# A recurrence and a gated two-layer network in one kernel: engines of 453 elementwise steps and the order of all steps read from two tables

## The chip, the cores and the metric

The kernel runs on one core of one Trainium2 chip. The core has a matrix engine (TensorE, PE in the rows; its weight loads are PEld), three elementwise engines (VectorE = DVE, ScalarE = ACT, GpSimd = POOL) and a queue that starts transfers (SyncE = SP). The metric is the device time of one execution in microseconds; lower is better.

## The reference

Per head, a state of 48 x 48 is decayed and updated once per position and read by a query; the result, brought to 3072 tokens of 384, goes through two matrix products with an activation between them. All inputs and outputs are float32.

```python
def _attn_ref(q, k, v, f_logit):                    # 4, 8, 768, 48
    f = 1.0 / (1.0 + np.exp(-f_logit))
    for t in range(S):
        state = f[:, :, t, :, None] * state + np.einsum('bhd,bhe->bhde', k[:, :, t], v[:, :, t])
        y[:, :, t] = np.einsum('bhd,bhde->bhe', q[:, :, t], state)
...
def _moe_ref(x, w_in, w_out):                       # 3072 x 384, 384 x 2048, 2048 x 384
    h = x @ w_in
    sp = np.where(h > 20.0, h, np.log1p(np.exp(np.minimum(h, 20.0))))
    g = h * np.tanh(sp)
    return g @ w_out
```

## The kernel before

**The recurrence** is done in 24 chunks of 128 positions (numbered n; one chunk holds half of the heads of two batches, and four chunks in a row make up one group of 512 tokens). `prep` makes the decays of a chunk (clamp, exp and ln on ACT, running sums on PE for chunks 0 to 2 and by a scan on DVE after that), and multiplies k by `inv` and q by `dec`, in `times`. `attn0` makes the scores and masks them into `a`; `attn1` transposes k into `kt`; `attn2` makes the two halves of the state update, of which `mid` and `tmp` are the results in the middle and at the end of the chunk; `attn3` and `outputs_of` make the outputs, and `evict` brings them to `xt` (group 0 goes through `xs`, which lies in the space named spareh) and decays the state on POOL.

**The network** is done in 98 units (numbered u): for one group of 512 tokens and one of 16 blocks of 128 hidden columns, PE makes `h` (L317; L327 for the first five blocks, where weights and tokens are not split into two parts), a chain of elementwise steps makes `g` from `h`, and PE adds `g` times the second weights into `o` (L365; L330 for the first blocks). The chain of `mish` is: exp (ACT, L351), clamp and add (DVE, L352), square (DVE, L344; ACT, L343, for the first 24 units), ln and exp (ACT, L354 and L355), `g` (DVE, L356, which also reads `h`), a copy `gh` into the short float type fp32r (ACT, L358) and the rest `gl` (POOL, L348; DVE, L347, for the first 24 units). PE multiplies `gh` and `gl` apart, so that products keep float32's precision. `h` has two buffers, so the product of unit u+2 waits until the step `g` of unit u has read its `h`; the output product of a unit is issued two units after its `h`.

**The weights** come as 64-bit words with the value in all of them. `load_w` brings a block of them together with one step on ACT (L476) and three on DVE (L478, L479, L481), and `split_w` splits it into `wh` (ACT, L493) and `wl` (DVE, L494). All 16 blocks are converted once, during the first third of the program.

**The order.** The kernel does not run its steps as it makes them. Each call of `plan.add` records a step with its engine, an assumed cost and the buffers that it reads and writes; there are 1813 steps. `Plan.order` packs them with a list scheduler that honours engines, buffers and the port that DVE and POOL share (`port`), perturbs the ranks with some 300 seeds of `MOVES`, and keeps the best. `Plan.issue` then writes the instructions out in the order of the planned starts. Each engine works off its own instructions strictly in that order. While PE is planned to wait, in the beginning, `issue` puts in a multiplication of zeros that keeps the engine busy (`idle`, L462); there are 26 of them, each of which shows as two matmuls in the rows.

## Time and profile before

| | us |
|---|---|
| median of 3 runs | 486.04 |
| lowest, highest | 484.88, 486.46 |
| the profiled execution | 484.71 |
| its span, first to last instruction | 482.9 |

1.8 us of the profiled execution lie around its span, and it is 1.33 us (0.27%) under the median. The clock of TensorE was granted in full (0.996 over the span), so no stretch is told apart by it. A row of windows gives the busy time of each engine in a stretch of the span; a row of a timeline gives start, duration, engine, line, output and inputs, and in brackets how long the engine stood idle just before and what released it. Durations of neighbours on DVE and ACT overlap by some 0.08 us, so what an instruction costs its queue is the distance from its start to the start of the next, where nothing waits between them.

### The profile page before, as it was taken

The numbers are of one execution on the slowest core, as the hardware profiler recorded it, in microseconds if no ns is written. First come the engines' busy times: TensorE is split into PE (matmuls) and PEld (weight loads), VectorE is DVE, ScalarE is ACT, GpSimd is POOL, SyncE is SP. The second block draws the span as 40 slices with busy tenths as digits, with TensorE's granted clock in tenths as the row PEclk, the third lists the DMA queues.
The fourth block names the chain that finished last, engine by engine and source line by source line (L and its number), as shares of the span: only waits on it lengthen the run. The fifth ranks groups of instructions, "written<-read, shape, count | busy, mean of one in ns | idle before, by whom it ended". The sixth has DMA issues, their size and how long they took to land.

```text
span 482.9 us, 12157 instructions
## 1 busy us (share of the span) xinstructions
PE 464.4 (96%) x5032; PEld 391.2 (81%) x5032; DVE 343.8 (71%) x600; ACT 352.8 (73%) x662; POOL 144.3 (30%) x126
## 2 busy tenths in 40 slices
PE   8988989899999999999999999999999999999994
PEld 8766547787778888888888888888888888888883
DVE  4579999999996878777676766865875554554551
ACT  6779887999989677667777787677676466665650
POOL 0411120000013354343543443343333233342431
PEclk9999999999999999999999999999999999999998
DMA  7776656453402253421211240220230000010001
GB/s 246 226 252 222 222 183 220 140 178 118 160 36 89 93 188 106 154 70 63 89 50 73 88 139 16 90 88 33 90 110 1 3 12 23 1 65 0 1 0 71
DMA packets 17102, 48.42 MB, mean 100 GB/s; under 512 B 2000, under 2 KB 2000, under 8 KB 17040
## 3 DMA queue, kind: packets, MB, share of 16 engines
q1 hardware_dynamic: 17040, 47.59, 28.9%
q8 instruction: 40, 0.66, 0.5%
q14 instruction: 22, 0.18, 0.1%
HBM read 39.32 MB, written 6.29 MB: 94 GB/s over the span
## 4 chain that ended last, share of the span: by engine, by line
PE 71%; DVE 13%; ACT 12%; issue 3%; DVEq 0%; ACTq 0%
PE o L365 30%; PE h L317 30%; DVE wt L479 2%; PE at L755 2%; DVE ng L356 2%; ACT ng L354 2%; PE at L762 1%; ACT ng L355 1%; ACT ng L343 1%; DVE wl L494 1%; PE at L609 1%; DVE gl L347 1%; ACT wt L476 1%; PE o L462 1%; PE h L582 1%
## 5 line engine op out<-in xcount | busy, mean ns | idle before, releaser
L317 PE MATMUL h<-xt,wh 128*128 128x512 f32 x546 | 164.2, 382 | 3.7 <-DVE ng L356 3.7
L348 POOL TENSOR_TENSOR gl<-ng,gh 128x512 fp32r<-128x512 f32 x74 | 100.6, 1362 | 174.4 <-ACT gh L358 153.4
L317 PEld LDWEIGHTS h<-xt,wh 128*128 128x128 f32 x546 | 101.6, 189 | 21.3 <-DVE ng L356 7.0
L356 DVE SCALAR_TENSOR_TENSOR ng<-ng,h 128x512 f32<-128x512 f32 x91 | 62.1, 684 | 63.6 <-ACT ng L355 63.0
L365 PE MATMUL o<-gh,wh 128*128 128x512 f32 x273 | 106.3, 389 | 0.0
L365 PE MATMUL o<-gl,wh 128*128 128x512 f32 x273 | 103.6, 379 | 0.5 <-DVE gl L347 0.5
L317 PE MATMUL h<-xt,wl 128*128 128x512 f32 x273 | 103.5, 379 | 0.0
L365 PE MATMUL o<-gh,wl 128*128 128x512 f32 x273 | 103.5, 379 | 0.0
L354 ACT ACTIVATE ng<-ng 128x512 f32<-128x512 f32 (+1 forms) x98 | 60.7, 620 | 35.3 <-DVE ng L344 31.1
L351 ACT ACTIVATE ng<-h 128x512 f32<-128x512 f32 (+1 forms) x98 | 57.3, 585 | 31.9 <-PE h L317 30.9
L358 ACT ACTIVATE gh<-ng 128x512 fp32r<-128x512 f32 x91 | 56.6, 625 | 22.3 <-PE o L365 14.6
L352 DVE TENSOR_SCALAR ng<-ng 128x512 f32<-128x512 f32 (+1 forms) x98 | 47.9, 489 | 30.0 <-ACT ng L351 29.5
L355 ACT ACTIVATE ng<-ng 128x512 f32<-128x512 f32 (+1 forms) x98 | 60.6, 619 | 2.4
L411 POOL TENSOR_TENSOR in<-in,inv 128x512 f32<-128x512 f32 x20 | 24.9, 1244 | 119.6 <-ACT inv L548 119.5
L365 PEld LDWEIGHTS o<-gl,wh 128*128 128x128 f32 x273 | 51.6, 189 | 8.2 <-DVE gl L347 0.9
L365 PEld LDWEIGHTS o<-gh,wh 128*128 128x128 f32 x273 | 51.6, 189 | 7.9 <-issue 0.2
L317 PEld LDWEIGHTS h<-xt,wl 128*128 128x128 f32 x273 | 51.6, 189 | 7.3
L365 PEld LDWEIGHTS o<-gh,wl 128*128 128x128 f32 x273 | 51.6, 189 | 6.8 <-issue 0.2
L344 DVE TENSOR_TENSOR ng<-ng 128x512 f32<-128x512 f32 x74 | 54.7, 739 | 2.2
L542 DVE TENSOR_TENSOR_SCAN inv<-gate,state 128x516 f32<-128x516 f32 x20 | 24.6, 1228 | 2.3 <-ACT gate L533 2.1
L780 POOL TENSOR_TENSOR state<-tmp,ends 128x192 f32<-128x192 f32 x20 | 14.7, 735 | 19.0 <-PE at L755 7.9
L479 DVE SCALAR_TENSOR_TENSOR wt<-raw,wt 128x768 int32<-128x768 int32 x16 | 17.9, 1119 | 0.2
(147 smaller groups left out, 571.7 us busy)
## 6 DMA issues: line engine op xcount, KB each, us to landing
in<-lk SPq DMA_DIRECT2D x18, 512.0 KB, 4.4
raw<-ww SPq DMA_DIRECT2D x12, 768.0 KB, 4.2
in<-qv SPq DMA_DIRECT2D x18, 512.0 KB, 4.2
out<-ob SPq DMA_DIRECT2D x18, 256.0 KB, 2.1
raw<-ww SPq DMA_DIRECT2D x8, 384.0 KB, 4.4
in<-lk SPq DMA_DIRECT2D x8, 256.0 KB, 3.6
in<-qv SPq DMA_DIRECT2D x8, 256.0 KB, 4.2
xt<-xt SPq DMA_DIRECT2D x15, 128.0 KB, 3.0
```

The lines of the kernel that those rows point to most:

```text
L317: nc.tensor.matmul(h, w[:, a * P : (a + 1) * P], read(xt[:, x, a], part), start=(n == 0), stop=(n == 3 * NK - 1))
L344: ("dve", T_DVE(w), 1, lambda: nc.vector.tensor_tensor(n, n, n, ALU.mult))
L348: ("pool", T_POOL(w), 1, lambda: nc.gpsimd.tensor_tensor(gl, g, gh.bitcast(F32), ALU.subtract))
L351: ("act", T_ACT(w, True), 0, lambda: nc.scalar.activation(n_out, h, AF.Exp)),
L352: ("dve", T_DVE(w / 2), 1, lambda: nc.vector.tensor_scalar(n, n, E_CAP, 1.0, ALU.min, ALU.add)),
L354: ("act", T_ACT(w), 0, lambda: nc.scalar.activation(g, n, AF.Ln, bias=0.5, scale=0.5)),
L355: ("act", T_ACT(w), 0, lambda: nc.scalar.activation(g, g, AF.Exp, scale=-1.0)),
L356: ("dve", T_DVE(w), 0, lambda: nc.vector.scalar_tensor_tensor(g_out, g_in, 1.0, h, ALU.subtract, ALU.mult)),
L358: ("act", T_ACT(w), 0, lambda: nc.scalar.activation(gh, g, AF.Copy)),
L365: nc.tensor.matmul(o, w, read_again(x), start=(first and i == 0), stop=(last and i == 2))
L411: add("pool" if on_pool else "dve", cost, lambda: eng.tensor_tensor(dst, x, y, ALU.mult), reads, writes, port=port)
L479: add("dve", T_DVE(W_TILE), lambda: nc.vector.scalar_tensor_tensor(t, low, 29, t, ALU.logical_shift_right, ALU.bitwise_or), [kr], [kt], po ...
```

## The change

The list scheduler and its seeds are gone. `Plan.order` reads the order of all 1813 steps from a table, `ORDER`, and keeps only the arithmetic of planned starts, on which the fillers of `issue` depend. A second table, `CHOICES`, has one digit for each of 453 steps that may run on one of two engines; `Plan.either` takes the engine from it. Such steps are the square, `gh` and `gl` of each unit, `wh` and the split of `xs`, the two products of `times` (q only from chunk 9 on), the copies out of PSUM (`kt`, `mid`, `xs`, the upper part of `xt`) and the decay of the state. 187 of them stand on another engine than before, the greatest groups being these:

| step | from | to | count |
|---|---|---|---|
| square | DVE | ACT | 45 |
| `gh` | ACT | DVE | 43 |
| `gl` | POOL | DVE | 34 |
| `gl` | DVE | POOL | 9 |
| k or q product | POOL | DVE | 9 |
| k or q product | DVE | POOL | 10 |
| copies out of PSUM | ACT | DVE | 25 |
| decay of the state | POOL | DVE | 7 |

The rest are two of `wh`, one copy of the split of `xs` and two squares of the first 24 units, from ACT to DVE. The assumed costs of `load_w` are raised for blocks 6 to 15. The arithmetic is the same on all inputs.

```diff
+ORDER = (
+    0, 1, 35, 60, 110, 36, 85, 61, 175, 86, 11, 2, 12, 3, 13, 4, 14, 5, 15, 17, 6, 7, 8, 16, 9, 19, 18, 24, 10, 37,
...
+CHOICES = (
+    "1000010101000000001000100110000111000010000001001000000010000100010000100100100000000001001001100110"
...
+    def either(self, options, reads, writes):
+
+        n = len(self.open)
+        self.open.append((len(self.steps), options))
+        engine, cost, port, issue = options[int(CHOICES[n]) if n < len(CHOICES) else 0]
+        self.add(engine, cost, issue, reads, writes, port=port)
...
-        square = (
-            ("act", T_ACT(w), 0, lambda: nc.scalar.activation(n, n, AF.Square)) if early else
-            ("dve", T_DVE(w), 1, lambda: nc.vector.tensor_tensor(n, n, n, ALU.mult))
+        def prefer(first, second, other):
+            return (second, first) if other else (first, second)
...
+        high = prefer(
+            ("act", T_ACT(w), 0, lambda: nc.scalar.activation(gh, g, AF.Copy)),
+            ("dve", T_DVE(w / 2), 1, lambda: nc.vector.tensor_copy(gh, g)),
+            not early,
+        )
+        low = prefer(
+            ("dve", T_DVE(w), 1, lambda: nc.vector.tensor_tensor(gl, g, gh.bitcast(F32), ALU.subtract)),
+            ("pool", T_POOL(w), 1, lambda: nc.gpsimd.tensor_tensor(gl, g, gh.bitcast(F32), ALU.subtract)),
+            not early,
+        )
...
+        def copy(cols, dst, src, reads, writes):
+
+            plan.either((
+                ("act", T_ACT(cols, True), 0, lambda: nc.scalar.activation(dst, src, AF.Copy)),
+                ("dve", T_DVE(cols), 0, lambda: nc.vector.tensor_copy(dst, src)),
+            ), reads, writes)
...
+            late = j >= 6
...
-            add("act", T_ACT(W_TILE) + 65, lambda: nc.scalar.activation(
+            add("act", T_ACT(W_TILE) + 80 + 320 * late, lambda: nc.scalar.activation(
...
-            add("dve", T_DVE(W_TILE), lambda: nc.vector.scalar_tensor_tensor(
+            add("dve", T_DVE(W_TILE) + 220 * late, lambda: nc.vector.scalar_tensor_tensor(
                 t, low, 29, t, ALU.logical_shift_right, ALU.bitwise_or), [kr], [kt], port=True)
```

Three places show how the instructions move. The first is ACT some 14 us into the program. `in1` and `h0` hold chunk 1, `spareh` and `o0` chunk 2, `raw0` to `wt0` is the first step on the first block of weights, and `mid0<-at2` is the middle state of chunk 1. Before:

```order
L548 ACTIVATE h0_108<-h0_108 128x512
L789 ACTIVATE spareh_63<-at1_106 128x2x64
L612 ACTIVATE kt0_85<-at2_107 128x512
L555 ACTIVATE ends_72<-h0_108 128x4
L548 ACTIVATE o0_110<-o0_110 128x512
L789 ACTIVATE spareh_63<-at1_106 128x2x64
L555 ACTIVATE ends_72<-o0_110 128x4
L789 ACTIVATE spareh_63<-at0_105 128x2x2x64
L476 ACTIVATE wt0_103<-raw0_101 128x768
L688 ACTIVATE mid0_88<-at2_107 128x64x3
```

The same place now:

```order
L566 ACTIVATE h0_108<-h0_108 128x512
L488 ACTIVATE wt0_103<-raw0_101 128x768
L573 ACTIVATE ends_72<-h0_108 128x4
L566 ACTIVATE spareh_63<-o0_110 128x512
L566 ACTIVATE o0_110<-o0_110 128x512
L420 ACTIVATE kt0_85<-at2_107 128x512
L573 ACTIVATE ends_72<-o0_110 128x4
L420 ACTIVATE spareh_63<-at1_106 128x2x64
L420 ACTIVATE mid0_88<-at2_107 128x64x3
```

The weights step stands seven places further ahead of the middle state, with chunk 2's exponentials, `kt` and the ends of two chunks between them, and two of the three copies into spareh have left for DVE.

The second is DVE before the step `g` of unit 10, which is the last row of each piece (`ng0<-ng0,h0`); `wt0`, `wt1` are blocks of weights in conversion. Before:

```order
L352 TENSOR_SCALAR ng0_93<-ng0_93 128x512
L494 TENSOR_TENSOR wl0_62<-sparel_64,wh0_61 128x768
L356 SCALAR_TENSOR_TENSOR ng0_93<-ng0_93,h1_109 128x512
L478 TENSOR_SCALAR wt1_104<-wt1_104 128x768
L479 SCALAR_TENSOR_TENSOR wt1_104<-raw1_102,wt1_104 128x768
L356 SCALAR_TENSOR_TENSOR ng0_93<-ng0_93,h0_108 128x512
```

The same place now:

```order
L493 SCALAR_TENSOR_TENSOR wt0_103<-raw0_101,wt0_103 128x768
L358 SCALAR_TENSOR_TENSOR ng0_93<-ng0_93,h1_109 128x512
L354 TENSOR_SCALAR ng0_93<-ng0_93 128x512
L491 SCALAR_TENSOR_TENSOR wt1_104<-raw1_102,wt1_104 128x768
L348 TENSOR_TENSOR gl0_98<-ng0_93,gh0_95 128x512
L493 SCALAR_TENSOR_TENSOR wt1_104<-raw1_102,wt1_104 128x768
L358 SCALAR_TENSOR_TENSOR ng0_93<-ng0_93,h0_108 128x512
```

The `gl` of unit 9 and the last join of a block's bits (L493), which came behind `g` of unit 10, now come ahead of it.

The third is POOL in the stretch in which the weights are converted, between the k products of chunks 8 and 10 (`in0<-in0,inv0`). Before, with the decay of chunk 7's state and k of chunk 9 between them, the second of which runs at 141 us:

```order
L411 TENSOR_TENSOR in0_81<-in0_81,inv0_84 128x512
L780 TENSOR_TENSOR state_73<-tmp1_90,ends_72 128x64x3
L411 TENSOR_TENSOR in1_82<-in1_82,inv0_84 128x512
L348 TENSOR_TENSOR gl0_98<-ng0_93,gh0_95 128x512
L411 TENSOR_TENSOR in0_81<-in0_81,inv0_84 128x512
```

The same place now:

```order
L414 TENSOR_TENSOR in0_81<-in0_81,inv0_84 128x512
L349 TENSOR_TENSOR gl1_99<-ng0_93,gh1_96 128x512 x2
L349 TENSOR_TENSOR gl2_100<-ng0_93,gh2_97 128x512
L349 TENSOR_TENSOR gl0_98<-ng0_93,gh0_95 128x512
L349 TENSOR_TENSOR gl2_100<-ng0_93,gh2_97 128x512
L349 TENSOR_TENSOR gl0_98<-ng0_93,gh0_95 128x512
L349 TENSOR_TENSOR gl2_100<-ng0_93,gh2_97 128x512 x2
L349 TENSOR_TENSOR gl1_99<-ng0_93,gh1_96 128x512
L349 TENSOR_TENSOR gl2_100<-ng0_93,gh2_97 128x512
```

The nine `gl` steps up to `gl1` of the last row but one (units 7, 10, 11, 12, 14, 15, 17, 20 and 22) have come from DVE to POOL, and the decay and the k product of chunk 9 have gone to DVE.

## Rows read from the trace of the kernel before

**Rows 1.** The page: busy time of each engine, share of the span, instructions.
```profile
PE 464.4 (96%) x5032; PEld 391.2 (81%) x5032; DVE 343.8 (71%) x600; ACT 352.8 (73%) x662; POOL 144.3 (30%) x126
```

**Rows 2.** Windows: busy time of each engine in five stretches of the span.
```profile
0.00:33.00 33.00, 29.37 (x645) 25.35 (x646) 19.10 (x45) 22.73 (x56) 8.23 (x16) 1.00 0.78 245
33.00:91.00 58.00, 52.84 (x818) 35.99 (x818) 55.18 (x94) 51.17 (x106) 9.13 (x9) 1.00 0.63 210
91.00:144.00 53.00, 50.44 (x230) 42.33 (x229) 51.57 (x77) 50.51 (x84) 1.48 (x1) 1.00 0.34 119
144.00:476.40 332.40, 331.73 (x3345) 287.57 (x3343) 217.83 (x387) 227.81 (x417) 125.43 (x100) 1.00 0.18 63
476.40:482.90 6.50, 0.00 (x0) 0.00 (x0) 0.08 (x1) 0.60 (x1) 0.00 (x0) 0.68 0.36 129
```

**Rows 3.** Windows of the fillers' line L462 alone: PE, PEld, clock, DMA.
```profile
0.00:33.00 33.00, 8.94 (x52) 7.95 (x52) 1.00 0.78 245
```

**Rows 4.** Waits of PE from 33 to 91 us: total, times, longest.
```profile
PE o L330 <- DVE ob L356: 1.8, 2, 1.2
PE at L738 <- POOL in L411: 1.0, 2, 0.6
```

**Rows 5.** Waits of PE from 91 to 144 us.
```profile
PE h L317 <- DVE ng L356: 2.2, 4, 1.0
```

**Rows 6.** Timeline of PE: the first product of unit 12.
```profile
90.56 0.70 PE L317 MATMUL h<-xt,wh 128*128 128x512 f32 x2 [0.21 <-DVE ng L356]
```

**Rows 7.** Timeline of DVE around the step `g` of unit 10.
```profile
87.41 0.68 DVE L356 SCALAR_TENSOR_TENSOR ng<-ng,h 128x512 f32<-128x512 f32 x1
...
89.84 0.67 DVE L356 SCALAR_TENSOR_TENSOR ng<-ng,h 128x512 f32<-128x512 f32 x1
90.43 0.67 DVE L347 TENSOR_TENSOR gl<-ng,gh 128x512 fp32r<-128x512 f32 x1
91.03 0.42 DVE L352 TENSOR_SCALAR ng<-ng 128x512 f32<-128x512 f32 x1
91.37 0.95 DVE L494 TENSOR_TENSOR wl<-wt,wh 128x768 fp32r<-128x768 f32 x1
92.24 0.69 DVE L347 TENSOR_TENSOR gl<-ng,gh 128x512 fp32r<-128x512 f32 x1
```

**Rows 8.** Timeline of DVE: the same conversion step of an early and a late block.
```profile
39.75 0.95 DVE L479 SCALAR_TENSOR_TENSOR wt<-raw,wt 128x768 int32<-128x768 int32 x1
...
108.50 1.17 DVE L479 SCALAR_TENSOR_TENSOR wt<-raw,wt 128x768 int32<-128x768 int32 x1
```

**Rows 9.** Timeline of ACT: `dec` of chunk 1, the first weights, `mid` of chunk 1.
```profile
14.31 0.59 ACT L548 ACTIVATE h<-h 128x512 f32<-128x512 f32 x1
...
17.94 0.90 ACT L476 ACTIVATE wt<-raw 128x768 f32<-128x768 f32 x1 [1.09 <-DMA raw<-ww]
18.74 0.31 ACT L688 ACTIVATE mid<-at 128x192 f32<-128x192 f32 x1
```

**Rows 10.** Timeline of SP: transfers up to the first weights (start, issuing time).
```profile
0.75 0.86 SPq L447 DMA_DIRECT2D in<-lk  x2
...
8.94 1.24 SPq L447 DMA_DIRECT2D in<-qv  x2
10.96 3.10 SPq L447 DMA_DIRECT2D raw<-ww  x2
```

**Rows 11.** Timeline of PE: scores of chunk 3, then `h` of unit 0.
```profile
26.00 0.69 PE L582 MATMUL at<-spareh 48*64 48x64 f32 x32
26.63 1.56 PE L327 MATMUL h<-spareh,sparel 128*128 128x256 f32 x6
```

**Rows 12.** Timeline of POOL and of DVE at 141 us.
```profile
141.34 1.48 POOL L411 TENSOR_TENSOR in<-in,inv 128x512 f32<-128x512 f32 x1 [66.69 <-ACT inv L548]
...
141.69 1.68 DVE L347 TENSOR_TENSOR gl<-ng,gh 128x512 fp32r<-128x512 f32 x1
```

**Rows 13.** The page: the group of POOL's `gl` steps.
```profile
L348 POOL TENSOR_TENSOR gl<-ng,gh 128x512 fp32r<-128x512 f32 x74 | 100.6, 1362 | 174.4 <-ACT gh L358 153.4 <-DVE ng L356 6.8 <-issue 3.2
```

More of the change, by code (lines that the diff above doesn't have):

```diff
@@ L73 @@
 IDLE = 1500.0
-COLD = 1000.0
 class Plan:
@@ new lines, in order @@
+    def order(self):
+        count = len(self.steps)
+        order = ORDER if len(ORDER) == count else range(count)
+        after = [[] for _ in self.steps]
+        for i, step in enumerate(self.steps):
+            for b in step[3]:
+                after[b].append(i)
+        free, ready, self.start = dict(self.FREE), [0.0] * count, [0.0] * count
+        transfers = shared = 0.0
+        for i in order:
+            e, cost, _, _, size, port = self.steps[i]
+            t = self.start[i] = max(free[e], ready[i], shared if port else 0.0)
+            end = free[e] = t + cost
+            if port:
@@ L156, in pack @@
                 shared = end
-                stale.update(("dve", "pool"))
-            if e == "sp" and not back:
-                transfers = max(transfers, end + 650.0) + steps[i][4] / 0.27
+            if e == "sp":
+                transfers = max(transfers, end + 650.0) + size / 0.27
                 end = transfers - 650.0
             for a in after[i]:
-                f = a if back else i
-                if engine[i] == engine[a] == "pe":
-                    lag = 0.0
-                else:
-                    lag = self.LATENCY[engine[f]]
-                    if back and engine[f] == "sp":
-                        lag += steps[f][4] / 0.27
-                ready[a] = max(ready[a], end + lag)
-                left[a] -= 1
-                if not left[a]:
-                    queue[engine[a]].append(a)
-                    stale.add(engine[a])
@@ L215, in issue @@
+                ready[a] = max(ready[a], end + (0.0 if e == self.steps[a][0] == "pe" else self.LATENCY[e]))
+        return order
     def issue(self):
@@ L687, in attn2 @@
             if n < B:
-                add("act", T_ACT(NP * D, True), lambda: nc.scalar.activation(mv, uv[0], AF.Copy),
-                    keys[:1], ["mid"])
+                copy(NP * D, mv, uv[0], keys[:1], ["mid"])
             else:
@@ L951, in recurrence_moe_kernel @@
                 )
-                for (e, c, shared, fn), (r, k) in zip(ops, rw):
-                    add(e, c, fn, r, k, port=shared)
+                for options, (r, k) in zip(ops, rw):
+                    if len(options) > 1:
+                        plan.either(options, r, k)
+                    else:
+                        e, c, shared, fn = options[0]
+                        add(e, c, fn, r, k, port=shared)
             while done < min(4 * NCH, attend_goal(u)):
```

150 lines of the change are left out of this document (42 added, 108 removed), and 107 rows, old and new, of tables (MOVES, ORDER).

## The prediction

> **What bounds the kernel now.** I began with the busy times. PE is busy for 464.4 of 482.9 us [rows 1], so the question is only what the remaining 18.5 us and the fillers are. Five windows tell where they lie [rows 2]. From 0 to 33 us PE is idle for 3.63 us and spends another 8.94 on multiplications of zeros [rows 3]. From 33 to 91 us it is idle for 5.16, from 91 to 144 for 2.56, from 144 to the last matmul for 0.67, and the last 6.50 us are eviction and transfer. After 144 us nothing but less PE work could help, and PE's work is the same in both kernels, apart from fillers. So the change is worth what it takes from the stalls before 144 us.
>
> Who is waited for there: PE's longest waits from 33 to 91 us are for DVE's step `g` (written to ob), then for POOL's k product [rows 4], and from 91 to 144 us for `g` again [rows 5]. DVE itself is busy for 55.18 of 58 and for 51.57 of 53 us [rows 2]: it is a full queue, and PE waits for the place that `g` has in it. Only before 33 us has DVE room: 19.10 us of 33 are busy. PE works in order, so its stalls don't add up freely. What counts is the latest point at which it is still held. One such point is the product of unit 12, held until 90.56 us [rows 6] by the `g` of unit 10, which starts at 89.84 [rows 7].
>
> **The change part by part.** Prices of DVE come from distances between starts [rows 7]: a step of 512 columns with two inputs 0.60 us (89.84 to 90.43), a tensor-scalar step of 512 columns 0.34 (91.03 to 91.37), a `wl` step of 768 columns 0.87 (91.37 to 92.24). Smaller tiles are scaled from these by columns; these are estimates.
>
> *DVE's queue up to `g` of unit 10.* Counting the rows of both orders up to that step, 16 come in and 2 go. (1) Ahead of `g` of unit 0, at some 32 us: the k product of chunk 1 (0.60), a cast `wh` (0.5), `mid`, four copies into xs and a decay (0.2 to 0.34 each, 1.6 in all), less half of chunk 0's k product (0.34): 2.4 us. (2) Ahead of `g` of unit 3, at some 46 us: a k product, a square and two copies, 1.5 us. (3) After that: a cast of the split of xs (0.34), a decay (0.27), the `gl` of unit 9 (0.60) and the last bit-join of a block of weights (1.1), less the `gl` of unit 7 (0.60): 1.7 us. Parts (1) and (2) fall where DVE stood idle, 13.9 us before 33 us and part of 2.8 us after it [rows 2], so I price them at nothing; if that cover fails they cost up to 3.9. Part (3) falls into a full queue: `g` of unit 10 comes 1.7 us later.
>
> A cast on DVE into fp32r has no row. Its ends are 0.34 and 0.60 for 512 columns [rows 7]; I take 0.34, since like the tensor-scalar step it has one input and both sides in SBUF. At 0.60 the two casts ahead of `g` of unit 10 cost 0.7 us more.
>
> *The chain of the first four chunks.* ACT stands still for 1.09 us until the first weights land at 17.94 us, and `mid` of chunk 1 goes behind them, at 18.74 [rows 9]. The weights' transfer starts to be issued at 10.96 us, behind the values of chunk 1 (8.94) and others [rows 10]. In the new order the transfer stands ahead of chunk 1's q and v and of half of the next ones. In bytes: 3.93 MB were asked for up to and with the weights, now 2.88. At the 245 GB/s of this stretch [rows 2] the missing 1.05 MB are 4.3 us, so the weights land at about 13.7. That is an added wait in ACT's queue too: the step now stands right behind `dec` of chunk 1, done in 14.9 [rows 9], with the ends, chunk 2's exponentials and `kt` queued behind it; landing at 13.7, it holds none of them. ACT had been free for `mid` of chunk 1 at 16.85 (17.94 - 1.09) and began it at 18.74, 1.9 us later; I take 1.4 of these, an estimate, as its update has to be over first. Beside that, the h of unit 0 now goes ahead of chunk 3's scores, which took 26.00 to 26.63 [rows 11]: 0.6 us. I take 2.0 us of gain for the chain. The ends: 3.1 us of gain, if the k product of chunk 1 on DVE and the nearer `dec` also pass through; 1.1 us of loss, if chunk 1's q, now behind the weights (0.26 MB more in front of it, 1.1 us at the same rate), sets the pace.
>
> *PE's side of the same point.* Three matmuls of an output product (0.66 us, at 50.44/230 = 0.22 each [rows 2]) now stand ahead of the product of unit 12: work done while it would have stalled. So PE's stall up to unit 12 changes by 1.7 - 2.0 - 0.66, about -1.0 us.
>
> *Behind unit 10.* From the `g` of unit 10 to that of unit 20 the rows of DVE come to 38.2 us at these prices in the order before, and PE's products between the two that wait for them to 36.5: DVE fell 1.7 us further behind, and these are the stalls up to 129 us. Now `gl` steps have gone to POOL (0.60 us each) and casts come in (0.34), and DVE has 33.5 us against the same 36.5: 3.0 us of room. So unit 10 is the last place that holds PE, and I let the 2.56 and 0.67 us of later stalls shrink to 1.2: -2.0 us. The ends are 0 and -3.2. The raised costs of late conversions add nothing by themselves; they say what the trace says (0.95 us early, 1.17 late [rows 8]), and the late blocks are priced so here.
>
> *After 144 us* 38 casts, 34 `gl` and 45 squares change places. DVE's 217.83 of 332.40 us rise by some 15, ACT's 227.81 fall [rows 2]: nobody is full, PE has the work of two units in hand, and the cost is nothing; it is up to 1.5 us, if `gl` or `gh` in a row's new place comes late now and then. The fillers are 30 instead of 26: at 8.94/26 = 0.34 us each, 1.4 us if none of them falls into a wait; I take 0, since there the chain and not PE sets the pace (3.63 us idle [rows 2]). The tail keeps its steps: 0.
>
> Sum: -1.0 - 2.0 = -3.0 us, a span of 479.9 and an execution of 481.7 by the profiled one, which is 1.33 us under the median. From the median of 486.04: **483.0 us**.
>
> **The rivals.** (A) *A larger gain.* If the first chunks' chain and the room before 46 us give more, `g` of unit 10 no longer holds PE, and all that is left are the stalls and fillers before 33 us. Then 5.16 + 2.56 us go: 478.3 us. For it speaks that every stall named in rows 4 and 5 is for one step in a queue that could be ordered otherwise; against it, that the new order puts 1.7 us more in front of just that step.
>
> (B) *The wait only moves.* The chain gains nothing, because chunk 1's q lands later while `mid` lands earlier, and unit 10 comes 1.7 us later: 1.7 - 0.66 - 2.0 = -1.0 us, 485.0, no difference that can be measured. A change below 0.3%, 1.46 us, is about what can't be told from none for this kernel.
>
> (C) *Slower: POOL holds DVE.* Beside a POOL step that started at 141.34 us and took 1.48, a DVE `gl` step took 1.68 us, where it took 0.69 alone [rows 7, 12]. A `gl` step on POOL takes 1.36 us on average [rows 13]. Between the `g` of units 10 and 20 there are now six of them beside DVE's full queue. In the order each has one or two DVE steps beside it that read `h` or `o` instead of two tiles in SBUF, so I count the hold as covered but for some 2.5 us, and the room of 3.0 us takes these. If every one holds DVE for its whole length, 8.2 us, DVE is 5.2 us behind at unit 20, where it fell 1.7 behind before; less the 1.0 gained up to unit 12, that is 2.5 us more stall: 488.5 us. It decides from 5.7 us of hold (3.0 + 1.7 + 1.0) of the 8.2. Against it speaks that `g`, which reads `h`, stands right behind most of them.
>
> The Trainium skill, "SBUF — State Buffer", section "Who interferes with whom", says of this that a DVE step with two inputs in SBUF, or one in a two-port mode, and a POOL step that reads SBUF exclude each other for the whole instruction, while a DVE step with at most one input in SBUF outside those modes goes on. By that rule (C) needs all its neighbours to be of the first kind; the step at 141 us, held to the end of POOL's and then as long as alone, agrees with the exclusion, and no row here shows how `g` fares.
>
> **How the numbers follow.** Forecast (a gain of 1.5 to 6 us): 0.57, since each of its two halves has a row of its own. (A) 0.14. (B) 0.15. (C) 0.14, with the failure of the cover before 46 us counted in. So faster by over 0.3%: 0.71; within: 0.15; slower: 0.14. The range: below, up to (A)'s 478.3, of which a part is left out; above, (B) and the cheaper half of (C), with the dear casts (0.7) and fillers (1.4): 478.5 to 487.0.
>
> **What would show it.** In the profile after: the first weights on ACT at about 13.7 us and `mid` of chunk 1 before 18; PE idle from 33 to 91 us by about 4 us and from 91 to 144 by under 1; `g` of unit 10 at about 89.5 us; casts `gh` on DVE at 0.42 us each; PE busy for all but 1 us of the stretch from 144 us to its last matmul. I am wrong if DVE has idle time in its conversion stretch beside POOL's `gl` (C), if chunk 1's q product waits for its transfer (B), or if new waits for `gl` or `gh` show after 144 us.

## The result, and the profile after

The changed kernel took 481.27 us (median of 5 runs, 480.82 to 482.86), the kernel before 485.52 on the same occasion: a ratio of 0.992, with a 95% interval of 0.9896 to 0.9945. Run a second time, beside the first experiments, it took 480.24 us (6 runs) to 486.23: 0.9877 (0.985 to 0.9904). The gain is thus 4 to 6 us, where 3.0 were forecast. The profiled execution took 482.38 us with a span of 480.6.

The answers to [rows 1, 2] are these, the busy line of the page and the same five stretches (busy time of PE, PEld, DVE, ACT, POOL; then granted clock, DMA share, GB/s):

```profile
PE 465.5 (97%) x5040; PEld 392.6 (82%) x5040; DVE 352.2 (73%) x659; ACT 347.2 (72%) x634; POOL 108.0 (22%) x95
```
```profile
0.00:33.00 33.00, 28.96 (x646) 25.38 (x646) 22.45 (x53) 21.87 (x53) 6.60 (x15) 1.00 0.77 240
33.00:91.00 58.00, 55.15 (x837) 37.78 (x826) 55.56 (x101) 50.40 (x99) 8.33 (x7) 0.97 0.65 213
91.00:144.00 53.00, 52.48 (x243) 44.75 (x242) 49.41 (x76) 49.15 (x82) 13.81 (x8) 1.00 0.35 119
144.00:474.50 330.50, 328.93 (x3329) 284.66 (x3327) 224.69 (x432) 225.15 (x402) 79.25 (x65) 1.00 0.18 64
474.50:480.60 6.10, 0.01 (x1) 0.00 (x0) 0.09 (x1) 0.60 (x1) 0.00 (x0) 0.83 0.38 137
```

Taken from the length of each stretch, PE's idle time is now 4.04 us before 33 us (it was 3.63), 2.85 up to 91 (5.16), 0.52 up to 144 (2.56) and 1.57 after that (0.67); about 4, under 1 and 1 were forecast for the last three. The tail is 6.10 (6.50). DVE now works for 22.45 us of the first 33, where it was 19.10, and has 3.6 us of room from 91 to 144 us, where it had 1.4. What is left of PE's waits, from 33 to 91, from 91 to 144 and from 144 us on (waiting line, releaser, total, times, longest), answering [rows 4, 5]:

```profile
PE h L319 <- DVE ob L358: 1.6, 1, 1.6
PE h L309 <- DVE ng L358: 0.8, 1, 0.8
PE at L755 <- POOL in L414: 0.4, 2, 0.3
...
PE h L309 <- DVE ng L358: 0.8, 1, 0.8
PE o L367 <- ACT ng L356: 0.5, 1, 0.5
...
PE h L309 <- DVE mid L708: 0.8, 1, 0.8
PE h L309 <- DVE ng L358: 0.6, 1, 0.6
```

The place on which the prediction rested barely moved. In the timelines of DVE and PE, `g` of unit 10 and the first product of unit 12 are at (start, duration, idle time ahead):

```profile
89.95 0.68 DVE L358 SCALAR_TENSOR_TENSOR ng<-ng,h 128x512 f32<-128x512 f32 x1
```
```profile
90.68 0.70 PE L309 MATMUL h<-xt,wh 128*128 128x512 f32 x2 [0.79 <-DVE ng L358]
```

They were at 89.84 and 90.56 [rows 6, 7], and 89.5 was forecast for the first. Ahead of them lies something that the profile of before doesn't have, a fall of the clock. The rows of after are the product of unit 4 in PE's timeline, the window around it, and DVE's next step for that unit:

```profile
44.51 4.54 PE L319 MATMUL h<-spareh,sparel 128*128 128x512 f32 x6 [1.59 <-DVE ob L358]
```
```profile
44.50:49.00 4.50, 4.49 (x9) 1.64 (x10) 3.57 (x6) 2.50 (x6) 0.00 (x0) 0.62 0.77 249
```
```profile
49.72 0.43 DVE L354 TENSOR_SCALAR ng<-ng 128x512 f32<-128x512 f32 x1 [1.65 <-ACT ng L353]
```

Right behind a wait of 1.59 us the granted clock is 0.62 of full speed, a mixture of 1.2 and 2.4 GHz. The six multiplications take 4.54 us; before they took 2.84. DVE's full queue stands still for 1.65 us because of it. So this one execution shows less of the change than it gives otherwise.

A ruler for the rest: the start of the 4th, 11th and 24th `g` step on DVE (units 3 and 10 are the first two), and the span, all from one profile for each kernel. Each ratio is taken to runs of the kernel before on the same occasion, whose medians lay between 485.4 and 486.2 us; so medians of different rows can be compared to about 1 us only.

| kernel | median us (runs) | ratio to before, 95% | 4th g | 11th g | 24th g | span |
|---|---|---|---|---|---|---|
| before | 485.52 (5) | 1 | 46.5 | 89.8 | 143.6 | 482.9 |
| after | 481.27 (5) | 0.992 (0.990 to 0.995) | 44.4 | 90.0 | 141.6 | 480.6 |
| again | 480.24 (6) | 0.988 (0.985 to 0.990) | 46.7 | 90.6 | 142.2 | 481.0 |
| order_only | 494.30 (6) | 1.017 (1.014 to 1.020) | 45.4 | 90.0 | 143.2 | 492.9 |
| engines_only | 496.52 (6) | 1.021 (1.019 to 1.024) | 46.0 | 89.9 | 147.5 | 493.3 |
| new_to_u26 | 483.05 (12) | 0.994 (0.991 to 0.997) | 44.8 | 88.7 | 140.3 | 481.1 |
| old_to_u4 | 482.01 (6) | 0.992 (0.990 to 0.994) | 46.4 | 90.1 | 141.8 | 480.6 |
| gl_on_dve | 483.15 (12) | 0.996 (0.994 to 0.998) | 43.9 | 88.4 | 140.6 | 479.0 |
| gl_all_pool | 483.16 (12) | 0.996 (0.994 to 0.998) | 42.7 | 87.4 | 140.6 | 478.3 |
| fill_u4 | 481.41 (12) | 0.993 (0.990 to 0.995) | 44.5 | 88.5 | 140.2 | 479.5 |
| q_ahead | 481.59 (6) | 0.993 (0.990 to 0.996) | 43.0 | 86.9 | 138.7 | 477.4 |
| u4_ahead | 480.19 (6) | 0.990 (0.987 to 0.994) | 42.2 | 86.0 | 137.7 | 476.7 |
| u10_ahead | 482.59 (9) | 0.995 (0.992 to 0.998) | 43.3 | 87.4 | 140.9 | 479.7 |
| three_moves | 480.13 (6) | 0.988 (0.985 to 0.990) | 44.6 | 88.4 | 140.1 | 478.6 |

### The profile page after: what moved, and what is told of

The parts are those of the page before. It is cut to its first block, busy times and chain, and to the rows that moved or that the text cites. A ratio compares the mean times of both kernels' runs of the same rounds, so it can differ in the third digit from the quotient of the medians.

```text
span 480.6 us, 12141 instructions
## 1 busy us (share of the span) xinstructions
PE 465.5 (97%) x5040; PEld 392.6 (82%) x5040; DVE 352.2 (73%) x659; ACT 347.2 (72%) x634; POOL 108.0 (22%) x95
## 4 chain that ended last, share of the span: by engine, by line
PE 77%; DVE 11%; DMA 5%; ACT 3%; issue 2%; SPq 0%; ACTq 0%; DVEq 0%
PE h L309 34%; PE o L367 34%; DMA raw<-ww 2%; DMA in<-qv 2%; PE at L772 2%; DVE wt L491 2%; PE at L779 1%; DVE inv L560 1%; PE at L627 1%; PE h L319 1%; DVE wl L509 1%; DVE ng L354 1%; PE h L600 1%; DMA spareh<-lk 1%; DVE ng L358 1%
## 5 line engine op out<-in xcount | busy, mean ns | idle before, releaser
L349 POOL TENSOR_TENSOR gl<-ng,gh 128x512 fp32r<-128x512 f32 x49 | 69.4, 1417 | 214.0 <-ACT gh L343 118.4
L309 PEld LDWEIGHTS h<-xt,wh 128*128 128x128 f32 x546 | 101.3, 189 | 19.8 <-DVE ng L358 3.3
L358 DVE SCALAR_TENSOR_TENSOR ng<-ng,h 128x512 f32<-128x512 f32 x91 | 62.2, 685 | 41.3 <-ACT ng L357 40.3
L354 DVE TENSOR_SCALAR ng<-ng 128x512 f32<-128x512 f32 (+1 forms) x98 | 45.0, 459 | 40.7 <-ACT ng L353 40.4
L356 ACT ACTIVATE ng<-ng 128x512 f32<-128x512 f32 (+1 forms) x98 | 60.7, 619 | 11.2 <-DVE ng L339 6.3
L357 ACT ACTIVATE ng<-ng 128x512 f32<-128x512 f32 (+1 forms) x98 | 60.7, 620 | 2.5
L367 PEld LDWEIGHTS o<-gh,wh 128*128 128x128 f32 x273 | 51.6, 189 | 9.3 <-ACT ng L338 0.9
L309 PEld LDWEIGHTS h<-xt,wl 128*128 128x128 f32 x273 | 51.6, 189 | 7.3
L367 PEld LDWEIGHTS o<-gl,wh 128*128 128x128 f32 x273 | 51.6, 189 | 7.3
L367 PEld LDWEIGHTS o<-gh,wl 128*128 128x128 f32 x273 | 51.6, 189 | 6.9 <-issue 0.2
L338 ACT ACTIVATE ng<-ng 128x512 f32<-128x512 f32 (+1 forms) x67 | 41.3, 617 | 17.6 <-DVE ng L354 17.4
L343 ACT ACTIVATE gh<-ng 128x512 fp32r<-128x512 f32 x48 | 29.8, 625 | 16.2 <-DVE ng L358 12.1
L348 DVE TENSOR_TENSOR gl<-ng,gh 128x512 fp32r<-128x512 f32 x42 | 30.4, 726 | 6.1 <-ACT gh L343 4.5
L560 DVE TENSOR_TENSOR_SCAN inv<-gate,state 128x516 f32<-128x516 f32 x20 | 26.6, 1330 | 1.0 <-ACT gate L551 0.7
L414 POOL TENSOR_TENSOR in<-in,inv 128x512 f32<-128x512 f32 x12 | 14.6, 1220 | 47.8 <-ACT inv L566 47.6
L344 DVE CAST gh<-ng 128x512 fp32r<-128x512 f32 x43 | 18.6, 433 | 4.6 <-PE o L367 1.9
```

Source lines behind the costliest of these rows:

```text
L309: nc.tensor.matmul(h, w[:, a * P : (a + 1) * P], read(xt[:, x, a], part), start=(n == 0), stop=(n == 3 * NK - 1))
L338: ("act", T_ACT(w), 0, lambda: nc.scalar.activation(n, n, AF.Square)),
L343: ("act", T_ACT(w), 0, lambda: nc.scalar.activation(gh, g, AF.Copy)),
L348: ("dve", T_DVE(w), 1, lambda: nc.vector.tensor_tensor(gl, g, gh.bitcast(F32), ALU.subtract)),
L349: ("pool", T_POOL(w), 1, lambda: nc.gpsimd.tensor_tensor(gl, g, gh.bitcast(F32), ALU.subtract)),
L354: (("dve", T_DVE(w / 2), 1, lambda: nc.vector.tensor_scalar(n, n, E_CAP, 1.0, ALU.min, ALU.add)),),
```

## The experiments

My theory from the two traces: the time comes from two places, the head (up to the 4th `g`) and the stretch behind unit 10, both through DVE's queue; a fall of the clock takes some of it back, in some executions.

**Order and engines apart.** One kernel has the new order and the old engines, the other the old order and the new engines:

```diff
 order_only:    ORDER as after
-CHOICES = as after
+CHOICES = the engine of each step in the kernel before
 engines_only:  CHOICES as after
-ORDER = as after
+ORDER = the order of the kernel before
```

> The new order, with every elementwise step on the engine it had before. Theory Q (DVE's queue sets the time): by the prices of the prediction DVE has 69.8 us up to the g of unit 10, where it has 73.7 after and 68.1 before, and from there to the g of unit 20 35.7 us against 36.5 of PE; so it is no slower than after and may be up to 3 us faster: 478.5 to 481.5 us. Rival F (order and engines fit only each other): ACT, which takes back the casts and copies, is late for the steps of the order, and most of the gain is lost: 484 to 487 us.

> The order of before, with every elementwise step on the engine it has after. Theory Q: DVE has 72.2 us up to the g of unit 10, 4.1 more than before, in a stretch where it was full; from there to unit 20 it has 36.1 us against 36.5 of PE, so the later stalls of 2 to 3 us go: 486 to 488.5 us. Rival E (the engines do it, the order is nothing): 481 to 483 us.

They took 494.30 and 496.52 us: each half by itself is 8 and 10 us slower than before, beyond what either theory gave. So the sums of DVE's queue, from which theory Q forecast 478.5 to 481.5, tell nothing about such a mixture. The ruler says where: order_only reaches the 24th `g` at 143.2 us, as before, and loses 10.4 us between there and the end (349.7 us against 339.3); engines_only is 3.8 us late at the 24th `g` and loses 6.6 more behind it. Windows of PE from 144 to 474 us in order_only and in engines_only, and the fillers' group in order_only:

```profile
144.00:474.00 330.00, 323.33 (x3294) 276.60 (x3293) 213.29 (x378) 220.90 (x409) 119.02 (x98) 1.00 0.19 64
```
```profile
144.00:474.00 330.00, 323.91 (x3297) 279.37 (x3298) 223.41 (x430) 223.81 (x406) 77.06 (x64) 1.00 0.19 64
```
```profile
L473 PE MATMUL o<-state 128*128 128x128 f32 x84 | 13.6, 304 | 1.1 <-DVE state L436 1.1
```

No elementwise engine is full there (DVE 213 and 223 of 330 us), yet PE is idle for 6.67 and 6.09 us, in many waits of 1.1 us at most for a `g`, a `mid` or a mark. The fillers of order_only show as 84 multiplications of 13.6 us (60 of 9.8 in after), 1.9 us of them behind 144 us, where after has none. Of its 10.4 us behind the 24th `g`, 6.0 are PE's idle time (6.67 against 0.66 before), 1.9 these fillers and 2.9 lie in PE's other work, which has no more matmuls than before (335.0 against 332.1 us); its tail is 0.4 shorter. What lengthens that work is left open. A step on another engine takes another time and has another queue ahead of it, so a row of the order that was just in time need no longer be; that is argued, as no run takes the waits apart step by step.

**Where along the program.** new_to_u26 has order and engines of after for the first 617 steps, up to the product of unit 26, and those of before for the rest; old_to_u4 has those of before for the first 199 steps, with its fillers, and those of after for the rest.

```diff
 new_to_u26:
-ORDER = A
+ORDER = A[:617] + the rest in the order of before     (CHOICES alike)
 old_to_u4:
-ORDER = A
+ORDER = B[:199] + the rest in the order of after      (CHOICES, fillers alike)
```

> Order and engines of after up to the product of unit 26 (at some 144 us), those of before from there on. By the prediction nothing is won or lost after 144 us: 481.3 us, as after. By the trace of after PE is idle for 1.57 us after 144 us, where it was 0.67 before: if that comes from the new order there, 480.4 us. Rival: the late part brings the gain, 483 us or more.

> Order, engines and fillers of before up to the product of unit 4, those of after from there on. Theory H2 (the head gives some 2 us): the g of unit 3 comes at 46.5 us as before, where it was 44.4 after, and by the full queue behind it the g of unit 10 43.9 us later, at 90.4; in executions without a fall of the clock the time is 2 us above after, 482 to 483, which is all that is left of the gain behind unit 10. Rival (the head gives nothing, all of the gain comes behind unit 4): as after, 480.5 to 481.5.

new_to_u26 took the rival's 483 us, but it gives no answer: the rest after its 24th `g` takes 340.8 us (after 339.0, before 339.3), and at the seam PE has a wait that neither parent has:

```profile
146.57 0.70 PE L293 MATMUL h<-xt,wh 128*128 128x512 f32 x2 [1.37 <-DVE ng L342]
```

That late part, uncut, is the same in both kernels to 0.3 us. old_to_u4 came out by theory H2's numbers. In its timeline of DVE the 4th and the 11th `g` are:

```profile
46.39 0.42 DVE L358 SCALAR_TENSOR_TENSOR ob<-ng,h 128x256 f32<-128x256 f32 x1 [0.93 <-ACT ng L357]
...
90.10 0.68 DVE L358 SCALAR_TENSOR_TENSOR ng<-ng,h 128x512 f32<-128x512 f32 x1
```

46.4 and 90.1 were expected at 46.5 and 90.4, and 482.01 us lie in the 482 to 483. The time alone would not decide it: the ratio to before is 0.992, as in the first runs of after, and 0.988 in again. With the old head the rest of the change still gives 3.6 us by the medians. What the new head adds is 2.3 us at the 4th `g` (median of the ten profiles with new order and engines there, some with an edit: 44.2 us, against 46.5), but these scatter from 42.2 to 46.7. The six runs of old_to_u4, all with a mean clock of 0.997 or 0.998, lie within 1.5 us.

**The scatter of the new head.**

> The changed kernel once more, beside the hybrids that share its chip. Theory D (a dip of the clock): in the profile of after, the granted clock is 0.63 from 44 to 48 us, right behind a wait of 1.59 us of PE for the g of unit 2; the product of unit 4 then takes 4.54 instead of 2.84 us, DVE stands still for 1.65 us behind it, and the execution is some 1.7 us longer. By D a profile with a clock of 0.999 or a granted clock of 1.00 from 44 to 52 us goes with 480.8 us and one with the dip with 482.4. Rival: the dip is hidden and the times of after scatter for another reason; then both come with 481.3 +- 0.8.

Theory D was right about the price and wrong about the place. From the 4th to the 11th `g` after takes 45.6 us and again, with no fall there, 43.9: the fall cost 1.7 us. The profiled run of again (482.87 us, mean clock 0.992) has no fall at 44 us, but one at 22. The rows are PE's timeline ahead of it and the window of the fall:

```profile
21.61 0.24 PE L743 MATMUL h<-a,in 64*32 64x64 f32 x1 [1.96 <-issue]
```
```profile
22.00:29.00 7.00, 7.00 (x144) 6.11 (x133) 3.51 (x7) 2.95 (x7) 1.27 (x1) 0.52 0.69 230
```

For 7 us the granted clock is 0.52, almost all at 1.2 GHz, behind a stall of 1.96 us that nothing in the profile releases, in the middle of one step; `g` of unit 0 then starts at 36.3 us and not at the 33.4 of after. Both executions of again at 0.997 took under 480. The twelve runs of new_to_u26, with the same head, go from 480.77 us at a mean clock of 0.999 to 487.26 at 0.987; but one at 0.998 took 483.18, so the clock is not all of the scatter.

Of the first wait at unit 4 I tried two covers. fill_u4 puts six fillers ahead of its product, u4_ahead moves the awaited step up on DVE:

```diff
 fill_u4, PE:
+L473 MATMUL o_112<-state_74 128x128 x6
 L319 MATMUL h_108<-spareh,sparel 128x512 x3
 u4_ahead, DVE:
 L354 TENSOR_SCALAR ng_93<-ng_93 128x256
+L358 SCALAR_TENSOR_TENSOR ob_94<-ng_93,h_108 128x256
 L519 CAST xt_91<-spareh 128x512
 L491 SCALAR_TENSOR_TENSOR wt_104<-raw_102,wt_104 128x768
 L547 TENSOR_SCALAR in_81<-in_81 128x512
-L358 SCALAR_TENSOR_TENSOR ob_94<-ng_93,h_108 128x256
```

> Six more fillers (multiplications of zeros, 0.21 us each) ahead of the product of unit 4, in front of which PE stood idle for 1.59 us after and the granted clock fell to 0.63. They fill the wait for the g of unit 2. Theory D: a fall of the clock there costs 1.7 us in the executions that have it; with the wait filled, PEclk stays 1.00 from 44 to 52 us, and the median is 0.5 to 1.5 us below that of after. Rival: the fall comes elsewhere, or costs nothing that unit 10 does not wait for anyway: as after, or up to 0.5 us slower, where the fillers overrun the wait.

> One step of the changed kernel moved: DVE's g of unit 2, for which the product of unit 4 waits (1.59 us after, 1.1 us in five other profiles with this order), goes ahead of a cast, a bit step on the weights (1.26 us) and a short step. Its inputs are there at 42.1 us and it ran at 44.05. Fillers and all else as after. Theory G (at the two points where PE is held, g stands too far back in DVE's queue): the wait of 1.1 to 1.6 us goes, product of unit 4 some 1.2 us earlier, but the three steps behind it come 0.3 us later in a queue that is full from there to unit 10: g of unit 10 as before, and the time within 0.5 us of after, 480.5 to 481.5; a fall of the clock at 44 us is gone. Rival: DVE's idle 1.6 us at 48 us (it waits for that product) goes too, g of unit 10 comes 1 us earlier, and so does the end: 479.5 to 480.

In both profiles the clock is 1.00 from 33 to 91 us and the wait for `g` at unit 4 is gone, but PE waits elsewhere: in u4_ahead 1.0 us for the weights of the next product (`sparel`), in fill_u4 1.5 us for ACT's `kt`, which lies at 37 us, ahead of the fillers, and so has nothing to do with them. The 4th `g` to the 11th takes 44.0 and 43.8 us; it takes 43.7 to 44.0 in every profile with the new order and engines that has neither a fall nor an edit in that stretch, so nothing behind it changed. fill_u4 still has three of twelve runs at a clock of 0.986 to 0.989 (483.8 to 485.7 us); where the clock fell in these no trace shows. By the median its rival holds. The median of u4_ahead, 480.19 us, lies between theory G's range and its rival's and can't be told from that of after; the early spans in its profile (476.7 us) come from its head, which reached `g` of unit 0 at 31.4 us with the same steps up to there.

**The first chunks.**

```diff
 q_ahead, DVE:
+L412 TENSOR_TENSOR in_82<-in_82,h_108 128x512
 L490 TENSOR_SCALAR wt_103<-wt_103 128x768
-L412 TENSOR_TENSOR in_82<-in_82,h_108 128x512
 q_ahead, ACT:
-L488 ACTIVATE wt_103<-raw_101 128x768
 L573 ACTIVATE ends<-h_108 128x4
 L566 ACTIVATE spareh<-o_110 128x512
 L566 ACTIVATE o_110<-o_110 128x512
 L420 ACTIVATE kt_85<-at_107 128x512
+L488 ACTIVATE wt_103<-raw_101 128x768
```

> In the first chunks the weights' first step on ACT goes behind kt of chunk 1, and DVE's first step on them behind chunk 1's q product; all else, the fillers too, as after. Theory H (the head's chain starts DVE's full stretch, and the early weights took the chain's gain): DVE stood idle for 2.38 us ahead of that weights step, ACT for 1.86; chunk 1's q product comes at 14.5 to 15 us instead of 15.95, its scores 1.0 us earlier, unit 0's product some 0.7 us earlier, and the time is 0.5 to 1 us below after. Rival B' (another wait, the issue stall of 1.4 to 2.0 us at 20 us or the next transfer, takes its place): unit 0's product at 26.7 us as before, and the time as after within 0.3.

The profile looks like theory H (span 477.4, 4th `g` at 43.0), but the 4th `g` of gl_all_pool, whose head is after's step for step, came at 42.7. The q product came at 14.02 us, some 1 us ahead of the other profiles, and bought nothing: chunk 1's scores start at 16.35, where the eight profiles with after's head have 15.6 to 16.7, and PE is at work (transposes, fillers) up to them. The median of 481.59 us speaks for the rival. Whether the place of the first weights matters can't be told under the scatter.

**The gl on POOL.**

```diff
 gl_on_dve (units 7, 10, 11, 12, 14, 15, 17, 20, 22):
-L349 POOL TENSOR_TENSOR gl<-ng,gh
+L348 DVE TENSOR_TENSOR gl<-ng,gh
 gl_all_pool (units 8, 9, 13, 16, 18, 19, 21):
-L348 DVE TENSOR_TENSOR gl<-ng,gh
+L349 POOL TENSOR_TENSOR gl<-ng,gh
```

> The changed kernel with nine gl steps (units 7, 10, 11, 12, 14, 15, 17, 20 and 22) back on DVE, at the places that they have in the order; all else, the fillers too, as after. Theory Q (DVE's full queue holds PE up to 144 us, POOL's gl relieve it): by the prices of the prediction DVE has 0.6 us more up to the g of unit 10 and its lead over PE's products is worst at unit 21, where it has 3.3 us more than PE, and not at unit 10 (1.8 after): 1.5 us slower than after, with PE idle by some 2 us from 91 to 144 us where it was 0.5. Rival C (POOL's gl hold DVE as long as DVE would have worked itself): no slower than after, or faster, since the holds of 1.3 to 2 us each are gone.

> The suspect of rival C doubled: the seven other gl steps of units 8 to 21 (8, 9, 13, 16, 18, 19, 21) go to POOL too, at their places in the order; all else as after. Theory Q: DVE has 1.2 us less up to the g of unit 10 and 3.0 less up to that of unit 20: up to 1.2 us faster than after, if no output product waits for a gl. Rival C: 16 steps of 1.3 to 2 us hold DVE, which has 5 us of room: 2 us or more slower, with DVE steps stretched beside them.

From the 11th to the 24th `g` before takes 53.8 us, and every kernel with the new order, the new engines and no edit there 51.6 to 51.8; gl_on_dve takes 52.2 and gl_all_pool 53.2. Up to the 11th `g` the edits of units 7, 8 and 9 count too: from the 4th `g` on gl_on_dve takes 44.5 us and gl_all_pool 44.7, where the unedited order takes 43.7 to 44.0. So the nine steps are worth 1.2 us, 0.6 on either side of unit 10, near the 1.5 of theory Q: by its prices the one `gl` ahead of unit 10 is 0.6 us, and behind it DVE would have 37.1 us against PE's 36.5. PE's idle time from 91 to 144 us is 0.86 us, though, and not 2. Seven more steps on POOL, which should have given DVE 4.2 us, made it slower by 0.8 up to unit 10 and by 1.5 behind it, the 2 us of rival C, though no product of PE waits for a `gl` from 91 to 144 us. The medians of the two kernels, 483.2 us both, scatter too much to tell them apart. Windows from the 11th to the 24th `g` in after, gl_on_dve and gl_all_pool, with 8, 0 and 13 `gl` on POOL (of the five busy times DVE's is the third, POOL's the last):

```profile
89.95:141.60 51.65, 50.40 (x230) 42.94 (x231) 48.16 (x74) 47.26 (x79) 13.81 (x8) 1.00 0.36 123
```
```profile
88.36:140.59 52.23, 50.60 (x228) 42.66 (x229) 51.13 (x82) 47.41 (x79) 0.00 (x0) 1.00 0.36 121
```
```profile
87.38:140.56 53.18, 51.05 (x231) 42.93 (x231) 49.10 (x69) 47.66 (x78) 20.61 (x13) 1.00 0.34 119
```

At 0.60 us each, eight `gl` fewer should take 4.8 us off DVE and take 3.0; thirteen should take 7.8 and take 2.0. So POOL's steps hold DVE for some 1.8 us in after and 5.8 in gl_all_pool. The groups of DVE from 33 to 144 us show on which steps: the clamp (L354) and a bit step on the weights (L493), in after and then in gl_all_pool (busy time, mean ns):

```profile
L493 DVE SCALAR_TENSOR_TENSOR wt<-raw,wt 128x768 int32<-128x768 int32 x8 | 9.3, 1166 | 0.0
L354 DVE TENSOR_SCALAR ng<-ng 128x512 f32<-128x512 f32 x21 | 9.3, 441 | 3.1 <-ACT ng L353 3.1
```
```profile
L354 DVE TENSOR_SCALAR ng<-ng 128x512 f32<-128x512 f32 x21 | 11.9, 566 | 1.2 <-ACT ng L353 1.1
...
L493 DVE SCALAR_TENSOR_TENSOR wt<-raw,wt 128x768 int32<-128x768 int32 x8 | 11.3, 1409 | 0.1
```

These two alone are held for 4.6 us more (2.6 and 2.0), more than the 4.2 that left DVE. That is rival C's mechanism, and it is the neighbour in the order that decides: `g` (L358), which reads `h`, keeps 682 to 684 ns in both. Over the whole of after, the twelve clamps of 128x512 that start well inside a POOL step end 0.28 to 0.33 us behind it, wherever they began; the 26 `g` that do so take 0.69 us at most, as alone.

**The place of unit 10, and the long scan.**

```diff
 u10_ahead, ACT: wh of block 8 behind the square of unit 10
-L506 ACTIVATE wh<-wt 128x768
 L343 ACTIVATE gh_95<-ng_93 128x512
 L338 ACTIVATE ng_93<-ng_93 128x512
+L506 ACTIVATE wh<-wt 128x768
 u10_ahead, DVE:
+L358 SCALAR_TENSOR_TENSOR ng_93<-ng_93,h_108 128x512
 L493 SCALAR_TENSOR_TENSOR wt_104<-raw_102,wt_104 128x768
-L358 SCALAR_TENSOR_TENSOR ng_93<-ng_93,h_108 128x512
```

> Two steps of the changed kernel moved: ACT's wh of block 8 goes behind the square of unit 10, and DVE's last bit step of block 9 (1.13 us) behind the g of unit 10. In the trace of after the chain of unit 10 (exp 85.67, clamp 86.88, square 87.66, ln 88.31, exp 88.98, g 89.95 us) loses 0.75 us behind wh and 0.34 at g. The product of unit 12 waits 0.79 us for it. Theory G: g of unit 10 about 1.0 us earlier, the wait at unit 12 gone, and with no other point holding PE up to 144 us the time is 0.8 us below after: 480.2. Rival N (the next late step holds PE: weights of block 8 or 9 or the g of unit 11, delayed by 0.7): the 0.8 us come back as a wait within the next 10 us, time as after.

Theory G fell: `g` of unit 10 came 44.1 us after the 4th, not a microsecond earlier. The rival was right that a wait comes within 10 us, but not for either step it named. The timelines of DVE and of POOL at that place, and a row of PE's waits from 91 to 144 us, in u10_ahead:

```profile
87.36 0.69 DVE L358 SCALAR_TENSOR_TENSOR ng<-ng,h 128x512 f32<-128x512 f32 x1 [1.13 <-ACT ng L357]
87.97 1.09 DVE L493 SCALAR_TENSOR_TENSOR wt<-raw,wt 128x768 int32<-128x768 int32 x1
88.98 1.49 DVE L354 TENSOR_SCALAR ng<-ng 128x512 f32<-128x512 f32 x1
```
```profile
88.85 1.34 POOL L349 TENSOR_TENSOR gl<-ng,gh 128x512 fp32r<-128x512 f32 x1 [12.91 <-ACT gh L343]
```
```profile
PE o L367 <- ACT ng L357: 1.6, 1, 1.6
```

DVE stood ready for 1.13 us: `g` waits for ACT's exponential, behind `gh` of unit 9 and my displaced `wh`. The queue of DVE and the chain through ACT end almost together there, and clearing the first alone gains nothing; the edit left `wh` in the second, only a step further on, so what both cleared would give is not tried. The clamp of unit 11 then met the `gl` on POOL, 0.13 us after it had begun, and took 1.49 us instead of 0.42; PE then waits 1.6 us at the end of that chain. A like meeting is in after, at another place, ahead of its wait of 0.8 us for `mid`. In three_moves that `gl` (unit 28) runs on DVE, behind `tmp`, beside the edits of q_ahead and u4_ahead.

```diff
 three_moves, DVE:
 L710 TENSOR_TENSOR tmp_89<-at_107,mid_88 128x64x3
+L348 TENSOR_TENSOR gl_99<-ng_93,gh_96 128x512
 three_moves, POOL:
-L349 TENSOR_TENSOR gl_99<-ng_93,gh_96 128x512
```

> Three small edits of the changed kernel together: those of q_ahead and of u4_ahead, and the gl of unit 28, which ran on POOL from 161.82 to 163.10 us, on DVE behind the middle state of that chunk. In the trace of after DVE's scan beside that gl takes 2.16 us; 18 of the 20 scans take 1.22 to 1.30, and the one other long scan (2.27 us at 240 us) also starts beside a gl on POOL. Behind it PE waits 0.80 us for DVE's mid at 165 us. Theory P (POOL's gl holds the scan): the scan takes 1.23 us, the wait of 0.8 us is gone, though DVE has 0.6 us more, and the time is 0.8 us below that of after at the same clock. Rival: the scan is long for its own place in the program (what stands ahead of it), and stays at 2.2. Of the other two edits I expect no more than their own runs showed, 0 to 1 us: 479 to 480.2 us, with the granted clock at 1.00 up to 91 us in the profile.

Timeline rows: DVE's scan and POOL's `gl` in after, then DVE's scan in three_moves:

```profile
162.03 2.16 DVE L560 TENSOR_TENSOR_SCAN inv<-gate,state 128x516 f32<-128x516 f32 x1
```
```profile
161.82 1.28 POOL L349 TENSOR_TENSOR gl<-ng,gh 128x512 fp32r<-128x512 f32 x1
```
```profile
160.53 1.23 DVE L560 TENSOR_TENSOR_SCAN inv<-gate,state 128x516 f32<-128x516 f32 x1
```

Theory P holds: with the `gl` away the scan takes 1.23 us and the wait of 0.8 us for `mid` is gone. The other long scan, which no edit touched, says the same: it began 0.10 us behind a `gl` in after and took 2.27 us; in three_moves it begins 0.16 us ahead of that `gl`, and POOL's step is the long one (DVE, then POOL):

```profile
238.16 1.23 DVE L560 TENSOR_TENSOR_SCAN inv<-gate,state 128x516 f32<-128x516 f32 x1
```
```profile
238.32 2.14 POOL L349 TENSOR_TENSOR gl<-ng,gh 128x512 fp32r<-128x512 f32 x1 [1.78 <-DVE gh L344]
```

The rival, that the scan is long for its place in the program, is out. In the time the 0.8 us don't show: the part behind the 24th `g` takes 338.5 us, against 338.8 to 339.0 in after, q_ahead and u4_ahead and 337.8 to 339.4 in all profiles with the new order and engines unedited there. The median of 480.13 us can't be told from the 480.24 of again. Its profile has a fall of the clock in the head too (0.95 over the first 33 us), against my expectation.

## Why the prediction was right

The sum was -3.0 us. By the ruler it was -2.3 in the head, +0.5 in the full queue, -2.1 behind unit 10 and -0.3 after that: -4.2. One term was too dear, and that another had the right size was luck, as its reason did not hold.

- **DVE's full queue up to unit 10.** The extra work ahead of 33 us was 3.35 us of DVE (2.4 priced), and nothing was paid for it: the cover held. Part (3) was over-sized. From the 4th to the 11th `g` DVE's work rose from 42.45 to 43.65 us (in q_ahead), by 1.2 and not 1.7, and the time by 0.3 to 0.6, since 0.94 us were idle before. This term is most of what the sum was too small by.
- **The cast.** 0.42 to 0.43 us long and 0.33 to 0.34 from start to start: the price taken, not the dear end. In after:

```profile
42.19 0.42 DVE L519 CAST xt<-spareh 128x512 fp32r<-128x512 f32 x1
42.53 1.26 DVE L491 SCALAR_TENSOR_TENSOR wt<-raw,wt 128x768 int32<-128x768 int32 x1
```

- **The chain of the first four chunks** was sized well (2.0 forecast, 2.3 found at the 4th `g`), but the gain lies at another place. The timelines of ACT, DVE and PE in after:

```profile
14.52 0.92 ACT L488 ACTIVATE wt<-raw 128x768 f32<-128x768 f32 x1 [1.86 <-DMA raw<-ww]
...
17.82 0.34 ACT L420 ACTIVATE mid<-at 128x192 f32<-128x192 f32 x1 [0.60 <-PE at L643]
```
```profile
15.47 0.56 DVE L490 TENSOR_SCALAR wt<-wt 128x768 int32<-128x768 int32 x1 [2.38 <-ACT wt L488]
15.95 0.68 DVE L412 TENSOR_TENSOR in<-in,h 128x512 f32<-128x512 f32 x1
```
```profile
26.67 1.46 PE L319 MATMUL h<-spareh,sparel 128*128 128x256 f32 x6
```

 One profile misleads here. The weights are late in this one (14.52 us), but the eight profiles with this head unedited have their step on ACT at 13.3 to 14.5, with a median of 13.7, as the bytes said, five of them without a wait. `mid` comes at 16.8 to 17.8 (median 17.4, before 18.74 [rows 9]): 1.3 us earlier where 1.4 were taken. The step that failed is the next one, that this and the 0.6 us of the scores reach the first product of unit 0. On DVE chunk 1's q product stands behind the weights and comes at 14.7 to 16.0 us (median 15.1, before 14.94), its scores at 15.6 to 16.7 (16.02), and unit 0 starts at 24.7 to 26.7 us (median 25.9 of the six with no fall of the clock ahead of it), where it was 26.63 [rows 11] and with the old order again 27.0 and 25.9 (old_to_u4, engines_only): 0.7 us of 2.0 at most, within the scatter. So up to unit 0 rival B was nearly right, though not for the transfer: in q_ahead that q product runs at 14.02. The sum had nothing for what follows. From the first product of unit 0 to the 4th `g` before takes 19.8 us and old_to_u4 19.4, and nine of the ten profiles with the new order and engines 17.2 to 17.7 (fill_u4, with its wait for `kt`, 18.8). There the waits for `o`'s `ob` of [rows 4] are gone. order_only takes 18.2 us, so the order gives some 1.6 of it without the engines; which steps do is not isolated.
- **PE's side** was counted rightly: without the fillers PE starts 1407 matmuls ahead of the product of unit 12 before and 1410 in after. These three and two more are missing behind the 24th `g` (3345 and 3340), so the gain shows there.
- **Behind unit 10**: -2.0 forecast, -2.1 found, in all eight profiles with no edit in that stretch to within 0.2; PE's idle time from 91 to 144 us is 0.52 (under 1 forecast). Of the two reasons named, `gl` on POOL carries 0.6 us; the order of DVE's steps, with the other changes of engine, the rest.
- **After 144 us**: 0 to +1.5 forecast, and about -0.3 found by the ruler. In after that is 0.9 more of PE's idle time (1.57 against 0.66 us), 0.8 less of its work, by the matmuls done ahead, and 0.4 less of tail. 0.8 of the 1.57 is one meeting of a `gl` with a scan: the size is inside what the forecast allowed for, but the reason it gave was a `gl` that comes late. DVE's work rose by 6.9 us and not by 15, which changes nothing, as DVE isn't full there.
- **Rival C** lost because of where the new order puts the `gl`, not because the hold is weak: some 1.8 us for eight steps in after, where 2.5 were allowed for six, but 5.8 for thirteen in gl_all_pool, and about 1.0 at single meetings (the clamp of u10_ahead, the two long scans of after). The Trainium skill, "SBUF — State Buffer", section "Who interferes with whom", has the rule that the prediction names, and what is seen here agrees with it: a scan with two inputs in SBUF (1.23 to 2.16 us) is held by a POOL step, `g` with one is not, and a clamp with one is (0.42 to 1.49 us), for which by that rule it has to be in a two-port mode; no row shows the mode.
- **The holding point** was half of it. u10_ahead shows that ACT's chain, with `wh` in it, holds unit 12 as late as DVE's queue does; a forecast that had moved only one of them would have failed.

## What to carry to other kernels

A sum over an engine's queue is worth trusting between two points where that engine is full and the order is given; it says nothing of a mixture of one order and another's engines, and half of such a pair can cost twice what the whole gains. Before work goes to POOL, look at which DVE step will stand beside it: a tensor-scalar step, a scan or a two-input step in SBUF that starts while POOL's runs is held to the end of it; `g`, which reads PSUM, is not. When a step moves on one engine, follow its whole chain to the next engines' queues, and read several profiles of the head of a kernel before crediting a microsecond there to an edit.
